# One int32 operation fewer in a reciprocal square root, and another choice of which score tiles VectorE exponentiates

## The chip, the cores and the metric

The kernel runs on one core of one Trainium2 chip. The time is that of the device, in microseconds, from the first to the last instruction and a little around it; lower is better. The engines that matter here are TensorE (PE in the profile; its weight loads are listed apart as PEld), ScalarE (ACT), VectorE (DVE), and SyncE (SP), whose queue issues the transfers.

## The reference

One block of a transformer on 2048 rows of 640 values in bfloat16: a layer norm, attention with 32 heads of 20 values each, a second layer norm, and a gated feed-forward layer of width 1728, each with its residual.

```python
def _layernorm(x, axis=-1, eps=1e-5):
    m = jnp.mean(x, axis=axis, keepdims=True)
    v = jnp.var(x, axis=axis, keepdims=True)
    return (x - m) / jnp.sqrt(v + eps)
...
        scores = jnp.einsum("bhqd,bhkd->bhqk", q, k) * (Dh ** -0.5)
        p = _softmax(scores, axis=-1)
        o = jnp.einsum("bhqk,bhkd->bhqd", p, v)
...
        h = _gelu(g) * u
        return jnp.einsum("bsf,fd->bsd", h, w_down)

    x = A_x
    h = x + _A_ref(_layernorm(x, axis=-1), A_wqkv, A_wo)
    h2 = h + _B_ref(_layernorm(h, axis=-1), B_w_gate, B_w_up, B_w_down)
```

The costly part is the softmax: 32 heads of 2048 x 2048 scores, each of which has to be exponentiated once. As tiles of 128 keys x 512 score columns that is 2048 tiles.

## The kernel before

**Chunks and slots.** The query rows are cut into seven chunks of 512, 512, 256, 256, 256, 128 and 128 rows (`CHUNKS`). The heads form eight groups of four. Attention is worked off in 32 slots of 64 score tiles each: a slot of chunk 0 or 1 is one group of heads, a slot of a 256-row chunk two groups, a slot of a 128-row chunk four. So slots 0 to 7 belong to chunk 0, 8 to 15 to chunk 1, 16 to 19, 20 to 23 and 24 to 27 to chunks 2, 3 and 4, 28 and 29 to chunk 5, and 30 and 31 to chunk 6.

**Units.** Within a slot, PE writes the scores of two or three tiles into neighbouring PSUM banks (function `unit`), and one ACT instruction exponentiates them together, 1024 or 1536 columns wide, into `pts` or `pts2` in SBUF. That is a unit. Two sets of banks are used in turn. A slot marked `2` in the string `PATS` alternates units of three tiles (banks 0 to 2) with units of two (banks 3 and 4). A slot marked `3` has units of three tiles in both sets (banks 0 to 2 and 3 to 5), and so takes bank 5 as well. Bank 6 gathers the product of probabilities and values. What is left, banks 7 and 5, or 7 alone in a slot marked `3`, serves all background work.

**VectorE's tiles.** In some units of three the third tile is not given to ACT but to VectorE (function `d_exp`). How many there are in each slot stands in the string `DS`, one hexadecimal digit per slot; they are spread evenly over the slot's three-tile units, leaving out the first and the last two. VectorE multiplies and clamps the 512 score columns into int16, which is a first approximation of the exponential's bfloat16 bits, and corrects them in a chain of seven operations over two such tiles at a time (over one, where a slot's number is odd). The product with the values then takes them up eight units later at the earliest.

**Background work.** Under all this run the projections of queries, keys and values (`proj`, `proj_v`), and for each finished chunk the function `post`: output projection, residual, layer norm statistics, `ln_rsqrt`, normalisation, transposes, the gate, the gelu, the up product and the down product. PE fills remaining time with matmuls that compute nothing (`idle`, from `gk`). Chunk 5 leaves its gelu, up and down work until the last exponential is done (`GT`). Chunk 6 has all its work after that: the tail.

**What sets the order.** `Sched` plans everything ahead with estimated durations and priorities: scores and their exponentials first, products with the values second, epilogues third, background last. The result is one fixed list of instructions for each engine, so each engine works strictly in that order, and an instruction whose input is late holds up all behind it. Any change of a number in `PATS` or `DS` gives a new plan for the whole kernel.

**The reciprocal square root.** `ln_rsqrt` has two branches. With `need_nm` (the first layer norm and the tail chunk) ACT takes a square root and VectorE a reciprocal. Without it (the second layer norm of chunks 0 to 5) VectorE does it alone for a chunk's one, two or four tiles of 128 rows at once: add epsilon, shift the bits right by one, subtract from a magic number, and two Newton steps of three operations each. That is nine operations on 1 to 4 columns.

Lines: most instructions go through the helper `I` and have line 386; 660 is a matmul in one piece (`whole`) and 664 one in four column groups (`quarters`); 618 and 952 are transposes; 749 copies projected values; 1081 copies gates, 1100 is the up product's multiplication and 1117 the down product's residual.

Of the kernel before, what the change touches and what calls it, by code (L numbers as in the profile page):

```python
# [6 lines left out]
ALU = mybir.AluOpType  # L7
# [3 lines left out]
I32 = mybir.dt.int32  # L11
# [39 lines left out]
class Sched:  # L51
# [10 lines left out]
    def op(self, eng, fns, dur, prio, reads=(), writes=(), acq=(), rel=(), after=(), sem=None, lat=None, mode=None, mb=0.0, alt=None):  # L62
        if self.evp is not None and eng == "dve" and rel and prio >= P_EPI:
            prio = self.evp
        o = Op()
        o.i = len(self.ops)
        o.eng, o.dur, o.lat, o.sem = eng, dur, LAT[eng] if lat is None else lat, sem
        o.mode = mode
        o.mb = mb
        o.alt = alt  # L70
        o.tag = writes[0] if writes else None
        o.fns = fns if isinstance(fns, list) else [fns]
        o.prio = (prio, o.i)
        deps = set(after)
        for r in reads:
            if r in self.lw:
                deps.add(self.lw[r])
        for w in writes:
            if w in self.lw:
                deps.add(self.lw[w])  # L80
            deps.update(self.rd.get(w, ()))
        for r in reads:
            self.rd.setdefault(r, []).append(o.i)
        for w in writes:
            self.lw[w] = o.i
            self.rd[w] = []
        deps.discard(o.i)
        o.deps = deps
        o.acq = list(acq)
        o.rel = list(rel)  # L90
        o.succ = []
        o.ready = 0.0
        o.start = None
        o.group = None
        self.ops.append(o)
        return o.i
# [230 lines left out]
RSQRT_MAGIC = float(0x5F3759DF)  # L327
# [25 lines left out]
XLAG = 0.85  # L353
XLG0 = 0.5
HG = 1
GT = (5,)
XPL = 1
KPR = 3.0
# [6 lines left out]
def bass_sequential_preLN__mha_block__glu_gated_geglu__prompt_kernel(  # L365
# [12 lines left out]
    with ExitStack() as es:  # L378
        sc = Sched(nc)
        op = sc.op  # L380
# [4 lines left out]
        def I(method, *args, **kwargs):  # L385
            return lambda eng: getattr(eng, method)(*args, **kwargs)  # L386


        def c_mm(n, passes=1):
            return 0.003 + passes * n / 2400.0  # L390
# [92 lines left out]
        def bank(b, n=512):  # L483
            return PS[:, 512 * b.b:512 * b.b + n]
# [91 lines left out]
        def ln_rsqrt(t0, n, prio, need_nm=0):  # L576
            ts = range(t0, t0 + n)
            y, v = rs[:, t0:t0 + n], mv[:, t0:t0 + n, 1]
            a, b = nw[:, 0, 0:n], nw[:, 1, 0:n]
            vk, rk = [("mv", t) for t in ts], [("rs", t) for t in ts]  # L580
            d = lambda fn, r, w: op("dve", fn, 0.14, prio, reads=r, writes=w)
            if need_nm:

                op("act", I("activation", a, v, ACT.Sqrt, bias=epsc[:, 0:1]), 0.19, prio, mode="sqrt", reads=vk + ["eps"], writes=["nw0", "sd"])
                d(I("reciprocal", y, a), ["nw0"], rk)
                if need_nm == 1:
                    d(I("scalar_tensor_tensor", out=nm[:, t0:t0 + n], in0=y, scalar=-1.0, in1=mv[:, t0:t0 + n, 0],
                        op0=ALU.mult, op1=ALU.mult), rk + vk, [("nm", t) for t in ts])
                return
            d(I("tensor_scalar", a, v, LN_EPS, None, ALU.add), vk, ["nw0"])  # L590
            d(I("tensor_scalar", b.bitcast(I32), a.bitcast(I32), 1, None, ALU.logical_shift_right), ["nw0"], ["nw1"])
            d(I("tensor_scalar", y.bitcast(I32), b.bitcast(I32), -1.0, RSQRT_MAGIC, ALU.mult, ALU.add), ["nw1"], rk)
            for _ in range(2):
                d(I("tensor_tensor", b, y, y, ALU.mult), rk, ["nw1"])
                d(I("scalar_tensor_tensor", out=b, in0=b, scalar=-0.5, in1=a, op0=ALU.mult, op1=ALU.mult),
                  ["nw0", "nw1"], ["nw1"])
                d(I("scalar_tensor_tensor", out=y, in0=b, scalar=1.5, in1=y, op0=ALU.add, op1=ALU.mult),
                  ["nw1"] + rk, rk)

        def ln_apply(eng, src, dst, dkey, t, rkeys, prio):  # L600
# [32 lines left out]
        def sc_id():  # L633
            _id[0] += 1
            return _id[0]
# [4 lines left out]
        for t0 in range(0, NT, 4):  # L640
            sa = [t for t in range(t0, t0 + 4) if LNS[t] == "act"]
            for t in range(t0, t0 + 4):
                (ln_stats_act if t in sa else ln_stats)(x_sb[:, t, :], t, [xkey(t)], P_EPI)
            if sa:
                assert sa == list(range(sa[0], sa[-1] + 1))
                op("dve", I("tensor_scalar", mv[:, sa[0]:sa[-1] + 1, 1], mv[:, sa[0]:sa[-1] + 1, 1], 1.0 / D, None, ALU.mult), 0.14,
                   P_QK, reads=[("mv1", t) for t in sa], writes=[("mv", t) for t in sa])
            ln_rsqrt(t0, 4, P_QK, 1)
            for t in range(t0, t0 + 4):
                e_ops.append(ln_apply(LNE[t], x_sb[:, t, :], xn_p[:, t % 4, :], ("xnp", t % 4), t, [xkey(t)], P_QK))  # L650
                transposes(xn_p[:, t % 4, :], [("xnp", t % 4)], xnT[:, :, t * 128:(t + 1) * 128], ("xnT", t),
                           ALLB, P_EPI, LNV[t])
                e_ops.append(len(sc.ops) - 2)
# [5 lines left out]
        def whole(out, l, r, start, stop):  # L659
            return [lambda eng: eng.matmul(out()[0:l.shape[-1]], l, r, start=start, stop=stop, skip_group_check=True)]  # L660

        def quarters(out, l, r, start, stop):
            m = l.shape[-1]
            return [lambda eng, j=j: eng.matmul(out()[j:j + 32], l[:, j:j + 32], r, start=start, stop=stop,  # L664
                                                tile_position=(0, j), skip_group_check=True) for j in range(0, m, 32)]
# [97 lines left out]
            tiles += [(s_, g, kb, j) for g in gs for kb in range(NT // nk) for j in range(4)]  # L763
            slot_end.append(len(tiles))

        PATS = '22222222222322232222222332223322'
        DS = '06418768558877797888786986867867'
        PAT = [((0, 1, 2), (3, 4, 5)) if PATS[i] == '3' else ((0, 1, 2), (3, 4)) for i in range(len(slots))]
        units, ubank, upos = [], [], []
        i = 0  # L770
# [154 lines left out]
        for s_, (c, gs) in enumerate(slots):  # L925
            us = [u for u, tl in enumerate(units) if len(tl) == 3 and all(x[0] == s_ for x in tl)]
            n = int(DS[s_], 16)
            us = us[1:len(us) - DTAIL]
# [50 lines left out]
        def post(c, banks, tail):  # L979
            p = P_EPI if tail else P_BG - PRE * (c >= PREC)  # L980
            q0, nq = CHUNKS[c]
# [10 lines left out]
            for tt in range(nt):  # L992
# [10 lines left out]
                for hf in range(2):  # L1003
                    bk = Bank(*banks)
# [11 lines left out]
            if tail:  # L1016
                op("act", I("activation", nm[:, 0:1], off0[:], ACT.Gelu_apprx_tanh), 0.06, -1, mode="gelu", reads=["off0"],
                   writes=["pre"], after=(sc.lw["sd"],))
# [5 lines left out]
            p, pre = P_BG - TFIRST * tail, p  # L1024
# [11 lines left out]
            def mms(k, w, wkey, after, p=p):  # L1036
                bk, key = Bank(*banks), ("bk", sc_id())
                for fi in range(min(fn_, NF - k * fn_)):
                    f = k * fn_ + fi
                    mf = min(128, DFF - 128 * f)  # L1040
                    for a in range(NA):
                        st = fi == 0 and a == 0
                        op("pe", quarters(lambda fi=fi: bank(bk)[:, fi * nq:(fi + 1) * nq], w[:, a, f * 128:f * 128 + mf],
                                          hnT[:, a, hb * 128:hb * 128 + nq], a == 0, a == NA - 1),
                           c_mm(nq), p, mode="col", alt=whole(lambda fi=fi: bank(bk)[:, fi * nq:(fi + 1) * nq],
                                                              w[:, a, f * 128:f * 128 + mf], hnT[:, a, hb * 128:hb * 128 + nq],
                                                              a == 0, a == NA - 1), reads=hk + [wkey], writes=[key], acq=[bk] if st else [],
                           after=after if st else ())
                return bk, key

            def wid(k):
                return min(512, NF * nq - 512 * k)
# [16 lines left out]
            else:  # L1069

                cp, gl = [], []
                for k in range(nb):
# [3 lines left out]
                    w_ = wid(k)  # L1076
                    if k >= nb - HG and c not in GT:
                        hold.append((k, bg, kg, m, fv, fk, w_))
# [3 lines left out]
                                 reads=[kg], writes=fk, rel=[bg], after=first))  # L1082
# [39 lines left out]

            if c in GT:
                def later(ba):
                    banks[:] = ba
                    gate_after[:] = [last_exp[0]]
                    rest()
                    down(GDP)
# [8 lines left out]
        if XPL:  # L1137
            op("act", I("activation", nm[:, 0:1], off0[:], ACT.Exp, scale=0.0), 0.06, P_QK, mode="exp", reads=["off0", ("xnT", 15), ("xnT", 14)],
               writes=["xpl", ("nm", 0)])
# [20 lines left out]
        for s_, (c, gs) in enumerate(slots):  # L1160
            if c == 0:
                g = s_
# [70 lines left out]
```

## Time and profile before

| | before |
|---|---|
| median of 3 runs | 939.43 us (938.72 to 939.80) |
| profiled execution, its own time | 939.73 us |
| its span, first to last instruction | 937.9 us |
| PE busy | 877.7 us (94%) |
| ACT busy | 904.2 us (96%) |
| DVE busy | 794.5 us (85%) |
| granted TensorE clock | 1.000 |

The profile's page lists busy times, groups of instructions by line, and who waited for whom. Two things have to be kept apart when it is read. The duration of an ACT instruction is longer than the time by which it moves its successor, because successive instructions overlap; the chain of work that ended last, in order of time, shows the latter. And an engine that is idle only costs time where it is the one on which the others depend at that moment. The slots can be found in the trace from the ACT instructions of 1024 and 1536 columns, which come in the units' order: slot 0 begins at 32.9 us, slot 31 at 880.4 us, and the last exponential ends at 908.4 us.

### The profile page before, as it was taken

The page shows a single profiled execution, that of the slowest core. Times are in us where ns is not written, and L with a number is a line of the kernel's source. Part 1 is how long each engine was busy: PE and PEld are TensorE (multiplying, and loading weights), DVE is VectorE, ACT ScalarE, POOL GpSimd, SP SyncE. Part 2 cuts the span into 40 slices and gives each one's busy share as a digit, 9 for nine tenths or more (in the row PEclk, how much of TensorE's full clock was granted, in tenths as well). Part 3 has the DMA queues.
Part 4 walks back from the last instruction along what each step waited for, and adds up shares of the span by engine and source line. Part 5 has one row for each costly group of instructions (what it writes and reads, how often), then busy time and mean ns, then how long its engine had stood idle before and what let it go on. Part 6 is the DMA issues. An engine that isn't in the chain of part 4 may idle for free.

```text
span 937.9 us, 33402 instructions
## 1 busy us (share of the span) xinstructions
PE 877.7 (94%) x15201; PEld 386.6 (41%) x15203; DVE 794.5 (85%) x1749; ACT 904.2 (96%) x884; POOL 11.2 (1%) x45
## 2 busy tenths in 40 slices
PE   5999999999999989999999999999889999989998
PEld 3433332222233222323343333344445654556666
DVE  8659768999999999688999996988998787898673
ACT  7999999999999999999999999999999999999891
POOL 4000000000000000000000000000000000000000
PEclk9999999999999999999999999999999999999999
DMA  7010000000000160000100000011000010000000
GB/s 253 2 30 2 2 1 2 1 1 2 1 2 2 33 253 2 1 1 17 43 3 1 2 2 2 2 31 26 7 3 3 3 31 17 17 4 3 5 18 15
DMA packets 11820, 19.90 MB, mean 21 GB/s; under 512 B 608, under 2 KB 9760, under 8 KB 11680
## 3 DMA queue, kind: packets, MB, share of 16 engines
q1 hardware_dynamic: 11680, 17.78, 5.7%
q8 instruction: 119, 1.95, 0.9%
q14 instruction: 21, 0.17, 0.1%
HBM read 15.16 MB, written 2.62 MB: 19 GB/s over the span
## 4 chain that ended last, share of the span: by engine, by line
ACT 74%; PE 20%; DVE 4%; POOL 1%; issue 1%; POOLq 0%
ACT pts L386 44%; ACT rege L386 29%; PE ps L664 7%; PE ps L386 7%; PE ps L660 4%; DVE rege L386 2%; PE ps L618 1%; POOL regw L386 1%; DVE stats L386 0%; DVE qt_all L386 0%; PE ps L952 0%; DVE rege L1100 0%; DVE kt_all L694 0%; ACT L1087 0%; ACT rege L1087 0%
## 5 line engine op out<-in xcount | busy, mean ns | idle before, releaser
L386 ACT ACTIVATE pts<-ps 128x1024 bf16<-128x1024 f32 (+1 forms) x482 | 549.3, 1345 | 3.2 <-PE ps L386 3.0
L386 ACT ACTIVATE rege<-ps 128x1024 bf16<-128x1024 f32 (+1 forms) x312 | 363.6, 1328 | 1.4 <-PE ps L386 1.3
L386 PE MATMUL ps<-qt_all,kt_all 32*128 32x256 bf16 (+2 forms) x3584 | 311.2, 288 | 36.1 <-ACT pts L386 16.4
L386 PEld LDWEIGHTS ps<-qt_all,kt_all 32*128 32x128 bf16 x3584 | 96.5, 92 | 275.8 <-ACT pts L386 130.6
L664 PE MATMUL ps<-rege,regw 128*32 128x256 bf16 (+2 forms) x2970 | 158.7, 308 | 5.1 <-issue 2.3
L386 PE MATMUL ps<-pts,v_all 128*21 128x256 bf16 (+2 forms) x1956 | 157.7, 292 | 0.4 <-DVE osb L386 0.3
L386 PE MATMUL ps<-rege,v_all 128*21 128x256 bf16 (+2 forms) x1394 | 129.4, 294 | 0.0
L664 PE MATMUL ps<-regw 128*32 128x512 bf16 (+1 forms) x1656 | 120.5, 358 | 1.0 <-DVE v_all L749 0.5
L386 DVE TENSOR_TENSOR rege<-rege 128x1024 bf16<-128x1024 bf16 (+3 forms) x170 | 108.4, 641 | 1.0
L386 DVE TENSOR_SCALAR qt_all<-ps 128x512 int16<-128x512 f32 x110 | 75.3, 685 | 16.0 <-PE ps L386 15.5
L664 PEld LDWEIGHTS ps<-rege,regw 128*32 128x32 bf16 x2970 | 73.3, 96 | 37.6 <-issue 17.5
L386 DVE TENSOR_SCALAR rege<-rege 128x1024 bf16<-128x1024 int16 (+3 forms) x225 | 87.3, 398 | 1.3
L386 DVE TENSOR_TENSOR qt_all<-qt_all 128x1024 bf16<-128x1024 bf16 (+3 forms) x124 | 82.3, 664 | 1.2
L664 PE MATMUL ps<-regw,rege 128*32 128x320 bf16 x1484 | 79.3, 301 | 0.3 <-DVE rege L1100 0.3
L386 DVE TENSOR_SCALAR rege<-ps 128x512 int16<-128x512 f32 x103 | 70.5, 684 | 9.0 <-PE ps L386 8.5
L386 DVE TENSOR_SCALAR qt_all<-qt_all 128x1024 bf16<-128x1024 int16 (+3 forms) x182 | 73.3, 408 | 1.9
L386 PEld LDWEIGHTS ps<-pts,v_all 128*21 128x21 bf16 x1956 | 46.4, 90 | 60.6 <-issue 52.5
L386 PEld LDWEIGHTS ps<-rege,v_all 128*21 128x21 bf16 x1394 | 38.4, 90 | 42.1 <-issue 35.1
L386 PE MATMUL ps<-wo,gk 128*21 128x256 bf16 x296 | 52.6, 274 | 0.0
L664 PEld LDWEIGHTS ps<-regw 128*32 128x32 bf16 x1656 | 37.8, 95 | 34.8 <-issue 15.9
L1100 DVE TENSOR_TENSOR rege<-rege,ps 128x512 bf16<-128x512 bf16 (+2 forms) x53 | 35.8, 676 | 13.1 <-PE ps L664 12.8
L664 PEld LDWEIGHTS ps<-regw,rege 128*32 128x32 bf16 x1484 | 35.8, 95 | 22.2 <-issue 13.7
(109 smaller groups left out, 727.3 us busy)
## 6 DMA issues: line engine op xcount, KB each, us to landing
rege<-in_A_x_dram SPq DMA_DIRECT2D x11, 320.0 KB, 4.7
out_dram<-rege SPq DMA_DIRECT2D x16, 160.0 KB, 1.9
regw<-in_B_w_gate_dram SPq DMA_DIRECT2D x1, 2160.0 KB, 9.2
regw<-in_B_w_up_dram SPq DMA_DIRECT2D x1, 2160.0 KB, 14.1
regw<-in_B_w_down_dram SPq DMA_DIRECT2D x1, 2080.0 KB, 19.2
rege<-in_A_wqkv_dram SPq DMA_DIRECT2D x1, 1600.0 KB, 9.0
rege<-in_A_x_dram SPq DMA_DIRECT2D x2, 640.0 KB, 4.4
regw<-in_A_wqkv_dram SPq DMA_DIRECT2D x1, 800.0 KB, 8.0
```

The lines of the kernel that those rows point to most:

```text
L386: return lambda eng: getattr(eng, method)(*args, **kwargs)
L618: op("pe", lambda eng, a=a: eng.transpose(bank16(bk, D)[:, 128 * a:128 * a + 128], src[:, a * 128:(a + 1) * 128], ident[:]), 0.056, prio, ...
L660: return [lambda eng: eng.matmul(out()[0:l.shape[-1]], l, r, start=start, stop=stop, skip_group_check=True)]
L664: return [lambda eng, j=j: eng.matmul(out()[j:j + 32], l[:, j:j + 32], r, start=start, stop=stop, tile_position=(0, j), skip_group_check=T ...
L1100: hdone.append(op("dve", lambda eng, bu=bu, fv=fv, m=m, w_=w_: eng.tensor_tensor(fv, fv, bank(bu, w_)[0:m, :], ALU.mult), c_dve(w_), p, re ...
```

## The change

In `ln_rsqrt` the shift and the subtraction from the magic number become one operation: the bits, taken as a number, times -0.5 plus the magic number. This branch has eight operations instead of nine.

`PATS` marks slots 12 and 22 with `3` that were `2`, and slot 29 with `2` that was `3`: seven slots of three-tile units instead of six. `DS` changes in ten slots: 1 (6 to 3), 2 (4 to 5), 10 (8 to 9), 13 (7 to 8), 15 (9 to 8), 20 (7 to 8), 22 (6 to 7), 24 (8 to 7), 27 (6 to 8) and 31 (7 to 8). In all VectorE takes 216 tiles instead of 213.

Three options are added and stay off: `LNG` (parts of the square root on GpSimd) with its `LNGT`, and `FW` (chunk 5's gates in one piece). With both at 0 the instructions they guard are those of before.

```diff
+LNG = 0
+LNGT = 0.2
+FW = 0
...
             d(I("tensor_scalar", a, v, LN_EPS, None, ALU.add), vk, ["nw0"])
-            d(I("tensor_scalar", b.bitcast(I32), a.bitcast(I32), 1, None, ALU.logical_shift_right), ["nw0"], ["nw1"])
-            d(I("tensor_scalar", y.bitcast(I32), b.bitcast(I32), -1.0, RSQRT_MAGIC, ALU.mult, ALU.add), ["nw1"], rk)
+            d(I("tensor_scalar", y.bitcast(I32), a.bitcast(I32), -0.5, RSQRT_MAGIC, ALU.mult, ALU.add), ["nw0"], rk)
+            if LNG:
+                g = lambda fn, r, w: op("pool", fn, LNGT, prio, reads=r, writes=w)
+            else:
+                g = d
             for _ in range(2):
-                d(I("tensor_tensor", b, y, y, ALU.mult), rk, ["nw1"])
-                d(I("scalar_tensor_tensor", out=b, in0=b, scalar=-0.5, in1=a, op0=ALU.mult, op1=ALU.mult),
+                g(I("tensor_tensor", b, y, y, ALU.mult), rk, ["nw1"])
...
+                g(I("scalar_tensor_tensor", out=b, in0=b, scalar=-0.5, in1=a, op0=ALU.mult, op1=ALU.mult),
                   ["nw0", "nw1"], ["nw1"])
-                d(I("scalar_tensor_tensor", out=y, in0=b, scalar=1.5, in1=y, op0=ALU.add, op1=ALU.mult),
+                g(I("scalar_tensor_tensor", out=y, in0=b, scalar=1.5, in1=y, op0=ALU.add, op1=ALU.mult),
                   ["nw1"] + rk, rk)
...
-        PATS = '22222222222322232222222332223322'
-        DS = '06418768558877797888786986867867'
+        PATS = '22222222222332232222223332223222'
+        DS = '03518768559878787888887976887868'
...
-                        op("pe", quarters(lambda fi=fi: bank(bk)[:, fi * nq:(fi + 1) * nq], w[:, a, f * 128:f * 128 + mf],
+                        wh = FW and c in GT
+                        op("pe", (whole if wh else quarters)(lambda fi=fi: bank(bk)[:, fi * nq:(fi + 1) * nq], w[:, a, f * 128:f * 128 + mf],
                                           hnT[:, a, hb * 128:hb * 128 + nq], a == 0, a == NA - 1),
-                           c_mm(nq), p, mode="col", alt=whole(lambda fi=fi: bank(bk)[:, fi * nq:(fi + 1) * nq],
+                           c_mm(nq), p, mode="full" if wh else "col", alt=None if wh else whole(lambda fi=fi: bank(bk)[:, fi * nq:(fi + 1) * nq],
```

More of the change, by code (lines that the diff above doesn't have):

```diff
@@ L590, in ln_rsqrt @@
             d(I("tensor_scalar", a, v, LN_EPS, None, ALU.add), vk, ["nw0"])
-            d(I("tensor_scalar", b.bitcast(I32), a.bitcast(I32), 1, None, ALU.logical_shift_right), ["nw0"], ["nw1"])
-            d(I("tensor_scalar", y.bitcast(I32), b.bitcast(I32), -1.0, RSQRT_MAGIC, ALU.mult, ALU.add), ["nw1"], rk)
-            for _ in range(2):
-                d(I("tensor_tensor", b, y, y, ALU.mult), rk, ["nw1"])
-                d(I("scalar_tensor_tensor", out=b, in0=b, scalar=-0.5, in1=a, op0=ALU.mult, op1=ALU.mult),
+            d(I("tensor_scalar", y.bitcast(I32), a.bitcast(I32), -0.5, RSQRT_MAGIC, ALU.mult, ALU.add), ["nw0"], rk)
[3 more added lines that the diff above has]
+                g = d
+            for _ in range(2):
+                g(I("tensor_tensor", b, y, y, ALU.mult), rk, ["nw1"])
+                if LNG:
+                    g(I("tensor_tensor", b, b, a, ALU.mult), ["nw0", "nw1"], ["nw1"])
+                    g(I("tensor_scalar", b, b, -0.5, 1.5, ALU.mult, ALU.add), ["nw1"], ["nw1"])
+                    g(I("tensor_tensor", y, y, b, ALU.mult), ["nw1"] + rk, rk)
+                    continue
+                g(I("scalar_tensor_tensor", out=b, in0=b, scalar=-0.5, in1=a, op0=ALU.mult, op1=ALU.mult),
                   ["nw0", "nw1"], ["nw1"])
-                d(I("scalar_tensor_tensor", out=y, in0=b, scalar=1.5, in1=y, op0=ALU.add, op1=ALU.mult),
+                g(I("scalar_tensor_tensor", out=y, in0=b, scalar=1.5, in1=y, op0=ALU.add, op1=ALU.mult),
                   ["nw1"] + rk, rk)
```

## The prediction

> **What bounds the kernel now.** I read the first part of the page, then who waited for whom on ACT between the first and last exponentials, then the chain of work in order of time, and last the busy times slot by slot.
>
> ```profile
> span 937.9 us, 33402 instructions
> PE 877.7 (94%) x15201; PEld 386.6 (41%) x15203; DVE 794.5 (85%) x1749; ACT 904.2 (96%) x884; POOL 11.2 (1%) x45
> ```
>
> ACT is the busiest engine. From 36.5 to 892 us its only waits for another engine are these (total us, times, longest):
>
> ```profile
> ACT pts L386 <- PE ps L386: 3.0, 3, 1.6
> ACT rege L386 <- PE ps L386: 1.3, 1, 1.3
> ```
>
> 4.3 us of 855: ACT sets the pace, and the attention phase ends when ACT has done its share of the 2048 score tiles. What a tile costs there is read from the chain (start, us, what), not from durations, because successive ACT instructions overlap:
>
> ```profile
> 98.55 2.75 ACT rege L386 x3
> 101.30 4.09 ACT pts L386 x4
> ...
> 114.01 3.60 ACT pts L386 x3
> ```
>
> Slot 2 begins at 89.8 and here has three 1024-column instructions in a row: 2.75 / 3 = 0.917 us each. The 4.09 holds three of these and one of 1536 columns: 4.09 - 2.75 = 1.34 us. Check: the 3.60 is one 1024 and two 1536, 0.917 + 2.68 = 3.60. The difference, 0.42 us, is one tile of 512; what remains of an instruction without its tiles is 0.917 - 0.84 = 0.07 us.
>
> The counts and durations by shape (us busy, mean ns):
>
> ```profile
> L386 ACT ACTIVATE pts<-ps 128x1024 bf16<-128x1024 f32 x322 | 347.3, 1202 | 1.6 <-PE ps L386 1.6
> L386 ACT ACTIVATE pts<-ps 128x1536 bf16<-128x1536 f32 x160 | 257.3, 1634 | 1.5 <-PE ps L386 1.4
> L386 ACT ACTIVATE rege<-ps 128x1024 bf16<-128x1024 f32 x225 | 245.4, 1208 | 1.4 <-PE ps L386 1.3
> L386 ACT ACTIVATE rege<-ps 128x1536 bf16<-128x1536 f32 x87 | 141.3, 1636 | 0.0
> ```
>
> 322 + 225 = 547 units of two tiles and 160 + 87 = 247 of three: 1094 + 741 = 1835 tiles, and 2048 - 1835 = 213 are VectorE's, the sum of the digits of `DS`.
>
> **Fewer tiles and instructions on ACT.** The new digits sum to 216, so ACT has 1832 tiles. The number of units follows from walking through the 64 tiles of each slot with the new pattern: a slot marked `2` takes 25.6 units, one marked `3` takes 21.3, and with seven marked `3` instead of six the walk gives 790 instead of 794. With n units of three, 3n + 2(790 - n) = 1832 gives n = 252, so 538 of two. ACT's change is 5 x 1.34 - 9 x 0.917 = 6.70 - 8.25 = -1.55 us. By the mean durations it would be 5 x 1.635 - 9 x 1.204 = -2.66; that counts overlap twice, so it is the far end of this term, and the near end is three tiles without any instruction saved, 3 x 0.42 = -1.26. I take -1.55, the chain's value.
>
> **Work put on VectorE.** A tile costs one operation on PSUM and its share of the chain of four `tensor_scalar` and three `tensor_tensor`:
>
> ```profile
> L386 DVE TENSOR_TENSOR rege<-rege 128x1024 bf16<-128x1024 bf16 x112 | 76.4, 684 | 0.8
> L386 DVE TENSOR_SCALAR qt_all<-ps 128x512 int16<-128x512 f32 x110 | 75.3, 685 | 16.0 <-PE ps L386 15.5
> ...
> L386 DVE TENSOR_SCALAR rege<-rege 128x1024 bf16<-128x1024 int16 x112 | 46.8, 419 | 1.0
> ```
>
> A chain over two tiles is 4 x 0.419 + 3 x 0.684 = 3.73 us. A further tile in a slot costs 0.69 us and, if it opens another pair, up to 3.73. Over the kernel there are 14 odd slots instead of 13 and 101 full pairs instead of 100, so VectorE gets 3 x 0.69 + 3.73 + at most 3.73, some 9.5 us. None of it is on the path while VectorE is in time. Whether it is, the busy times of the slots show (us of the slot, then PE, PEld, DVE and ACT busy with counts):
>
> ```profile
> 61.90:89.80 27.90, 25.93 (x372) 9.00 (x371) 24.57 (x54) 26.35 (x26) 0.00 (x0) 1.00 0.08 25
> 302.20:328.20 26.00, 24.57 (x256) 7.39 (x248) 25.29 (x52) 26.00 (x28) 0.00 (x0) 1.00 0.10 28
> 568.00:602.70 34.70, 32.73 (x542) 12.92 (x539) 26.75 (x53) 34.64 (x34) 0.00 (x0) 1.00 0.01 2
> 628.90:655.90 27.00, 26.54 (x541) 12.33 (x530) 22.38 (x57) 26.83 (x27) 0.00 (x0) 1.00 0.09 22
> 770.30:795.90 25.60, 25.22 (x564) 12.71 (x556) 19.36 (x37) 25.60 (x27) 0.00 (x0) 1.00 0.09 27
> 880.40:908.40 28.00, 25.66 (x857) 16.45 (x846) 21.71 (x46) 25.50 (x27) 0.00 (x0) 1.00 0.04 10
> ```
>
> These are slots 1, 10, 20, 22, 27 and 31. Where tiles are added VectorE is free for 7.9 us (slot 20), 4.6 (22), 6.2 (27, which gets two: 2 x 0.69 + 3.73 = 5.1) and 6.3 (31). Only slot 10 is full: 0.7 us free against 0.69 plus an added half chain. Its background copies wait into later slots, which I cost at nothing as long as scores don't need them.
>
> **The wait in slot 1.** The longest of ACT's waits stands at the end of slot 1:
>
> ```profile
> 89.83 2.37 ACT L386 ACTIVATE pts<-ps 128x1024 bf16<-128x1024 f32 x2 [1.58 <-PE ps L386]
> ```
>
> On PE and VectorE just before it:
>
> ```profile
> 88.94 0.40 PE L386 MATMUL ps<-rege,v_all 128*21 128x512 bf16 x4
> 89.15 0.32 PE L664 MATMUL ps<-regw 128*32 128x320 bf16 x4
> 89.40 0.40 PE L386 MATMUL ps<-qt_all,kt_all 32*128 32x512 bf16 x4
> ```
> ```profile
> 88.16 0.41 DVE L386 TENSOR_SCALAR rege<-rege 128x1024 int16<-128x1024 int16 x1
> ```
>
> The scores that ACT needs (89.40) stand in PE's list behind the slot's last products with values (88.94), and these need VectorE's chain, whose last operation ends at 88.57. VectorE was late because slot 1 had 24.57 us of work in 27.9. The change takes three of its six tiles, 3 x 0.69 + one pair and more, over 5.8 us. I take it that the chain is then done in time and the whole 1.58 us goes: -1.58. The bounds are 0 (the next late input is right behind it) and -1.58, since ACT had no work ready. What is late next there is PE itself, 25.93 us busy in 27.9; but slot 1 also has 1.3 us more of ACT's tiles, so PE gets that much longer.
>
> **The background's banks.** A slot marked `3` leaves the background one bank instead of two. What this costs PE can be read from the filler matmuls, busy time of those that read `gk` (first number after the slot's us; all fillers from slot 10 on):
>
> ```profile
> 352.90:379.40 26.50, 0.27 (x1) 0.09 (x1) 0.00 (x0) 1.00 0.00 1
> 491.40:517.30 25.90, 8.24 (x45) 3.44 (x45) 0.00 (x0) 1.00 0.01 2
> 628.90:655.90 27.00, 0.97 (x8) 0.61 (x9) 0.00 (x0) 1.00 0.09 22
> 795.90:822.30 26.40, 4.28 (x26) 2.01 (x26) 0.00 (x0) 1.00 0.06 16
> 822.30:847.20 24.90, 5.44 (x35) 2.73 (x34) 0.00 (x0) 1.00 0.02 4
> ```
>
> Slots 12 and 22, now `2`, have almost no filler; slots 28 and 29, now `3`, have 4.3 and 5.4 us. So turning a slot to `3` puts off some 4 us of PE's background work. Slot 12's is caught up in slot 17, where 8.24 us are filler. Slot 22's 3.3 to 4.5 us come back in slot 29, which turns to `2` and stops wasting 5.4. Net between -2 and +4 us of work left for the tail; I take 0, as the loss and the gain are of one size.
>
> **The square root.** One operation goes in each of six chunks:
>
> ```profile
> L386 DVE TENSOR_SCALAR nw<-nw 128x2 int32<-128x2 int32 x3 | 0.5, 163 | 0.0
> L386 DVE TENSOR_SCALAR nw<-nw 128x4 int32<-128x4 int32 x2 | 0.3, 160 | 0.0
> L386 DVE TENSOR_SCALAR nw<-nw 128x1 int32<-128x1 int32 x1 | 0.2, 154 | 0.0
> ```
>
> 6 x 0.16 = 1.0 us of VectorE in the background, hidden by ACT's exponentials; the tail's chunk takes the other branch. The merged operation is of the kind that stays, so it costs no more. I take 0 on the path, bounds 0 and -1.0. The options that stay off add nothing, and no transfer and no wait on SP or POOL moves.
>
> **PE's own stalls in the last slot.** ACT's other two long waits, in slot 31, follow gaps on PE in which it waited for no semaphore:
>
> ```profile
> 881.93 0.34 PE L664 MATMUL ps<-rege,regw 128*32 128x128 bf16 x9 [0.87 <-issue]
> ...
> 885.68 0.23 PE L664 MATMUL ps<-rege,regw 128*32 128x128 bf16 x1 [1.13 <-issue]
> ```
> ```profile
> 882.65 1.45 ACT L386 ACTIVATE pts<-ps 128x1536 bf16<-128x1536 f32 x1 [1.22 <-PE ps L386]
> ```
>
> The second costs ACT the 1.3 us of the waits above, so 2.5 together. They fall in a run of the shortest instructions, chunk 5's gates, 857 matmuls in slot 31 against 372 in slot 1, and that work stays there. I keep both: 0; bounds -2.5 and, if a third gap joins, +1.3.
> The Trainium skill (Runtime: NRT & Kernel Launch, section Instruction fetch mechanics) has PE's instructions fetched in blocks of 256 while the block before runs, and the crossing "mostly hidden". By that rule such gaps are no fixed price of short instructions, and the sum would be 2.5 us lower; the trace here leaves open which holds.
>
> **The sum.** 939.73 - 1.55 - 1.58 = 936.6 us, against the profiled execution, which lies 0.3 above the median of the runs; the runs spread by 1.1. I forecast 936.6.
>
> **The rivals.** (a) The wait in slot 1 stays or turns up at another slot's end, such as slot 10, where VectorE is full. For it: the pace is set by fixed lists, and one late input is enough. Against it: no other slot's end shows such a wait, slot 10's included. The time is 939.73 - 1.55 = 938.2. (b) The stalls of the last slot go with the new order as well: 936.6 - 2.5 = 934.1. For it: nothing but PE's own timing holds them there. Against it: the same short work falls in the same slots. (c) Slower: the bank taken in slots 12 and 22 leaves background for the tail, where it is in PE's way, since a part of the down products spills over already. From 908.4 us on PE runs
>
> ```profile
> L660 PE MATMUL ps<-regw,rege 128*128 128x320 bf16 x70 | 11.3, 300 | 0.5 <-DVE rege L1100 0.5
> ```
>
> 14 f-blocks by two halves are 28 for chunk 6 and 28 for chunk 5, so 14 of them, half a tile of rows and 2.3 us, are chunk 4's. If slot 22's 4 us come at the end in full, 936.6 + 4 = 940.6; if slot 12's 4 us come too, 944.6. It decides against the change once the spill passes 3.1 us, and can be measured as slower past 4.7 (936.6 + 4.7 = 941.3). Against it: slot 17's fillers and slot 29's second bank. That the change does not do what it says can't be: the counts follow from the strings.
>
> **How the numbers follow.** Chances: the forecast 0.45, (a) 0.24, (b) 0.17, (c) 0.14, with most of (c) past 941.3. About 0.2%, 1.9 us, can be told from no change: below 937.5 is faster, above 941.3 slower. Faster: the forecast and (b), 0.62, less a little for the forecast's own upper end: 0.60. Slower: 0.13. The same: 0.27. The range leaves out the far part of (c), 0.13, and a few in a hundred below: 933.4, which is every one of ACT's waits gone (939.73 - 1.55 - 4.3 = 933.9) and half of the square root's 1.0, up to 941.0.
>
> **What would show it.** Right: 538 ACT instructions of 1024 columns and 252 of 1536, 216 operations from PSUM to int16 on VectorE, no int32 shift; no ACT wait near 90 us; the last exponential some 3 us before 908.4 and a tail of 29.5 us as before. Wrong: ACT waits for scores at a slot's end elsewhere (a); PE's gaps gone or more (b); fewer fillers in slots 15 to 17, many more matmuls in the tail, which is longer by their time (c).

## The result, and the profile after

The changed kernel takes 937.39 us (median of 20 runs, 936.71 to 940.13) against 939.64 us for the kernel before, measured beside it. The ratio is 0.9979, with a 95% interval of 0.9973 to 0.9986: 2 us faster, a little more than can be told from no change. The forecast was 936.6. The profiled execution took 936.72 us, among the quickest of the 20, with a span of 934.9; so the profiles differ by 3.0 us and the medians by 2.25. One of the 20 runs of the kernel before took 3993.75 us, and one of 27 in a later round 1011.99; both are left out of the ratios.

The changed kernel's page, span and busy times, then ACT's waits between the first and the last exponential (total us, times, longest):

```profile
span 934.9 us, 33351 instructions
PE 876.2 (94%) x15171; PEld 385.8 (41%) x15173; DVE 798.1 (85%) x1760; ACT 902.4 (97%) x880; POOL 11.1 (1%) x45
```
```profile
ACT pts L389 <- PE ps L389: 1.3, 1, 1.3
ACT rege L389 <- PE ps L389: 0.9, 2, 0.5
```

ACT waited 4.3 us before and 2.2 now. Its exponentials by shape (the helper's line is now 389):

```profile
L389 ACT ACTIVATE pts<-ps 128x1024 bf16<-128x1024 f32 x331 | 358.2, 1220 | 1.4 <-PE ps L389 1.3
L389 ACT ACTIVATE pts<-ps 128x1536 bf16<-128x1536 f32 x154 | 250.6, 1661 | 0.1
L389 ACT ACTIVATE rege<-ps 128x1024 bf16<-128x1024 f32 x207 | 227.7, 1217 | 0.0
L389 ACT ACTIVATE rege<-ps 128x1536 bf16<-128x1536 f32 x98 | 159.2, 1666 | 0.9 <-PE ps L389 0.9
```

331 + 207 = 538 and 154 + 98 = 252, as worked out. The 1.58 us wait near 90 us is gone. What the scores behind it waited for, before (the weight load of these scores, then VectorE):

```profile
89.40 0.11 PEld L386 LDWEIGHTS ps<-qt_all,kt_all 32*128 32x128 bf16 x5 [0.34 <-DVE qt_all L733]
88.50 0.74 DVE L733 SCALAR_TENSOR_TENSOR qt_all<-ps,khalf,qt_all 128x512 bf16<-128x512 f32 x1
```

and after:

```profile
89.16 0.09 PEld L389 LDWEIGHTS ps<-qt_all,kt_all 32*128 32x128 bf16 x2 [0.27 <-DVE qt_all L744]
88.28 0.75 DVE L744 SCALAR_TENSOR_TENSOR qt_all<-ps,khalf,qt_all 128x512 bf16<-128x512 f32 x1 [0.36 <-PE ps L675]
```

They waited for the last operation on the next slot's queries (line 733, now 744), which stood in VectorE's list right behind the chain of its tiles. Slot 1 after (us of the slot, then PE, PEld, DVE, ACT busy):

```profile
61.90:89.60 27.70, 27.20 (x409) 9.75 (x401) 19.69 (x46) 27.57 (x27) 0.00 (x0) 1.00 0.07 25
```

VectorE has 19.69 us of work there instead of 24.57, and now waits 0.36 us for PE before that operation. So the queries are ready only 0.2 us sooner (89.03 instead of 89.24), and slot 2 begins at 89.6 instead of 89.8. The rest of the wait is filled, not saved in place: ACT has three tiles more to do in slot 1, 1.26 us, and fewer in other slots. The last exponential ends at 904.4 us instead of 908.4, 4.0 earlier; but the tail behind it takes 30.5 us instead of 29.5. In the chain of work in order of time (start, us, what), before:

```profile
909.49 1.06 PE ps L660 x7
910.54 0.45 PE ps L952 x4
```

and after:

```profile
905.68 1.67 PE ps L671 x10
907.36 0.44 PE ps L963 x4
```

The tail's first transposes (952, now 963) stand behind ten matmuls of chunk 4's down product instead of seven, and begin 2.96 us after the last exponential instead of 2.14. That is 0.8 of the 1.0 us.

### The profile page after: what moved, and what is told of

Its sections match the earlier page's. It is cut to its first block, busy times and chain, and to the rows that moved or that the text cites. A ratio compares the mean times of both kernels' runs of the same rounds, so it can differ in the third digit from the quotient of the medians.

```text
span 934.9 us, 33351 instructions
## 1 busy us (share of the span) xinstructions
PE 876.2 (94%) x15171; PEld 385.8 (41%) x15173; DVE 798.1 (85%) x1760; ACT 902.4 (97%) x880; POOL 11.1 (1%) x45
## 4 chain that ended last, share of the span: by engine, by line
ACT 83%; PE 12%; DVE 4%; POOL 1%; issue 1%; POOLq 0%
ACT pts L389 50%; ACT rege L389 32%; PE ps L671 4%; PE ps L675 4%; PE ps L389 3%; DVE rege L389 1%; DVE qt_all L389 1%; PE ps L629 1%; POOL regw L389 1%; DVE rege L1093 0%; DVE stats L389 0%; ACT L389 0%; ACT L1099 0%; PE ps L963 0%; ACT rege L1099 0%
## 5 line engine op out<-in xcount | busy, mean ns | idle before, releaser
L675 PE MATMUL ps<-rege,regw 128*32 128x256 bf16 (+2 forms) x2970 | 160.7, 308 | 3.4 <-DVE qt_all L744 0.8
L389 PE MATMUL ps<-rege,v_all 128*21 128x256 bf16 (+2 forms) x1396 | 127.5, 294 | 0.0
L389 DVE TENSOR_TENSOR rege<-rege 128x1024 bf16<-128x1024 bf16 (+2 forms) x172 | 111.7, 652 | 0.9
L389 DVE TENSOR_SCALAR qt_all<-qt_all 128x1024 int16<-128x1024 int16 (+3 forms) x187 | 74.0, 402 | 1.5
L675 PE MATMUL ps<-regw,rege 128*32 128x320 bf16 (+1 forms) x1452 | 71.9, 301 | 0.4 <-DVE rege L1129 0.3
L675 PEld LDWEIGHTS ps<-regw,rege 128*32 128x32 bf16 (+1 forms) x1452 | 35.0, 96 | 20.6 <-issue 9.9
```

## The experiments

What is compared throughout is the median and the ratio to the kernel before, measured on the same chip. Two numbers tell where time went: when the last exponential ends, and how many matmuls of 320 columns (down products) are left after it; 56 of them belong there, chunk 5's and 6's. Slot 0 begins between 32.5 and 33.7 us in these profiles, so a difference below 1 us in the fourth column says little by itself; and the intervals of the ratios are some 0.9 us to either side for most rows.

| kernel | us | ratio, interval | last exp. ends | 320-column matmuls after it |
|---|---|---|---|---|
| before | 939.6 | | 908.4 | 70 |
| changed | 937.4 | 0.9979 (0.9973 to 0.9986) | 904.4 | 78 |
| merged operation alone | 940.5 | 1.0010 (1.0001 to 1.0019) | 908.6 | 70 |
| new strings, old square root | 947.3 | 1.0083 (1.0069 to 1.0096) | 903.7 | 112 |
| merged, new PATS, old DS | 942.0 | 1.0026 (1.0016 to 1.0035) | 911.0 | 56 |
| merged, old PATS, new DS | 946.4 | 1.0073 (1.0061 to 1.0086) | 907.4 | 112 |
| changed, with six shifts more | 937.4 | 0.9983 (0.9974 to 0.9992) | - | - |
| changed, slot 29 as before | 938.5 | 0.9992 (0.9984 to 1.0001) | 905.8 | 94 |
| changed, slots 1 and 2 as before | 938.5 | 0.9984 (0.9975 to 0.9993) | 904.9 | 78 |
| changed, gates whole | 935.3 | 0.9956 (0.9943 to 0.9968) | 902.4 | 83 |
| before, gates whole | 937.1 | 0.9973 (0.9964 to 0.9983) | 906.2 | 73 |

**The merged operation alone.** The change's `ln_rsqrt` with the strings of before.

```diff
-        PATS = '22222222222332232222223332223222'
-        DS = '03518768559878787888887976887868'
+        PATS = '22222222222322232222222332223322'
+        DS = '06418768558877797888786986867867'
```

> The kernel before with the merged int32 operation alone; the strings PATS and DS as before. Chain theory (the step as predicted): VectorE has 1.0 us less work in the background under ACT, ACT has the same 794 instructions, the wait of 1.58 us near 88 us stays because chunk 0's square root comes only after slot 7. Ratio to before 0.9995 to 1.0005, within 0.5 us. Rival (the plan is what matters): six shorter operations give another plan from slot 8 on, and waits, PE gaps or the spill into the tail move by a microsecond or more: a ratio outside 0.999 to 1.001.

Measured: 940.5 us, ratio 1.0010 (1.0001 to 1.0019), on the edge between the theory's range and the rival's. One operation fewer did not make the kernel faster; by the medians it made it 0.9 us slower, barely clear of the noise. The new plan has two waits on ACT in slot 12 that the kernel before does not have:

```profile
357.52 1.02 ACT L389 ACTIVATE pts<-ps 128x1024 bf16<-128x1024 f32 x1 [0.34 <-PE ps L389]
359.35 1.02 ACT L389 ACTIVATE rege<-ps 128x1024 bf16<-128x1024 f32 x1 [0.80 <-PE ps L389]
```

**The strings alone.** The kernel before with the new PATS and DS.

```diff
-        PATS = '22222222222322232222222332223322'
-        DS = '06418768558877797888786986867867'
+        PATS = '22222222222332232222223332223222'
+        DS = '03518768559878787888887976887868'
```

> The kernel before with the new PATS and DS and the old nine-operation square root. Chain theory: the same 790 ACT instructions as in the changed kernel (538 and 252), slot 1's wait mostly gone, so all of the gain: ratio 0.9979 within 0.0007, last exponential ending 904 to 905.5 us. Rival (the strings were searched for the plan with the merged operation, and fit only that): the ratio lies nearer to 1, 0.999 or more, with waits in ACT after slot 8 that the changed kernel does not have.

Measured: 947.3 us, 7.7 us slower than before and nearly 10 slower than the changed kernel, from whose code it differs by one operation of 0.16 us in six chunks. The rival had the direction, but not the place: ACT's phase ends even earlier, at 903.7 us, and the loss stands in the tail (us busy, mean ns):

```profile
L660 PE MATMUL ps<-rege,regw 128*128 128x128 bf16 (+3 forms) x283 | 20.7, 229 | 0.0
L660 PE MATMUL ps<-regw,rege 128*128 128x320 bf16 x112 | 17.2, 300 | 0.0
```

Against 210 and 78 in the changed kernel: a good part of chunk 4's up product and all of its down product (56) are left over, and run on PE before and between chunk 6's own work. The background is late from chunk 1 on. That chunk's first normalisations in the changed kernel and in this one:

```profile
515.55 0.80 DVE L389 TENSOR_SCALAR xn_t<-rege,mv,rs 128x640 bf16<-128x640 bf16 x2
```
```profile
532.31 0.44 DVE L386 TENSOR_SCALAR xn_t<-rege,mv,rs 128x640 bf16<-128x640 bf16 x1
```

17 us late there, and not caught up: chunk 4's first normalisation comes at 849.1 us instead of 822.3.

**The operation's work, or the plan?** The changed kernel with the old pair of operations, the shift planned at no time, so that every engine's list stays and VectorE's has six shifts more.

```diff
-            d(I("tensor_scalar", y.bitcast(I32), a.bitcast(I32), -0.5, RSQRT_MAGIC, ALU.mult, ALU.add), ["nw0"], rk)
+            op("dve", I("tensor_scalar", b.bitcast(I32), a.bitcast(I32), 1, None, ALU.logical_shift_right), 0.0, prio, reads=["nw0"], writes=["nw1"], lat=-0.03); d(I("tensor_scalar", y.bitcast(I32), b.bitcast(I32), -1.0, RSQRT_MAGIC, ALU.mult, ALU.add), ["nw1"], rk)
```

> The changed kernel with the old pair of operations (shift, then -1.0 times and the magic number) put back, but the shift planned at a duration of zero, so that the lists of PE, ACT, POOL and SP stay as in the changed kernel and VectorE's list has six shifts more and is otherwise the same. Theory P (the plan decides, the operation itself is worth nothing): 937.4 us within 0.6, ratio 0.998, tail of 30 us. Theory W (the work decides: VectorE is so full that 1.0 us of it in the background costs many): near the 947 us of the kernel with the old square root and the new strings, at least 940.

Measured: 937.37 us against the changed kernel's 937.39. The traces show the same lists on PE (but for a few missing records), ACT and GpSimd, and on VectorE the same list with six shifts more. Theory P holds: the six operations cost nothing that can be measured (the interval is some 0.9 us to either side), and what the merged one does to the time it does through the plan. (The execution that was profiled took 940.15 us, far above this median; the last section shows what was different in it, and its two numbers are left out of the table.)

**One string at a time, both with the merged operation.** First the new PATS with the old DS, then the old PATS with the new DS.

```diff
-        DS = '03518768559878787888887976887868'
+        DS = '06418768558877797888786986867867'
```
```diff
-        PATS = '22222222222332232222223332223222'
+        PATS = '22222222222322232222222332223322'
```

> The merged operation and the new PATS with the old DS (213 tiles, one slot more with three-tile units). Chain arithmetic: three tiles more on ACT than in the changed kernel, +1.3 us, slot 1's wait back, +1.1: 939.8 us. If the plan decides: background that is early or late by more than that, 938 or less, or 941 or more, to be seen in the matmuls after the last exponential.

> The merged operation and the new DS with the old PATS (216 tiles, slots 12 and 22 of two- and three-tile units, slot 29 of three-tile units). Chain arithmetic: four ACT instructions more than in the changed kernel, +0.3 us: 937.7 us. If the plan decides: outside 936.7 to 938.7, to be seen in the matmuls after the last exponential.

Measured: 942.0 and 946.4 us. Both lie outside what the chain arithmetic gives, the second by nearly 9 us. With the new DS alone, chunk 4's whole down product is left over once more:

```profile
L671 PE MATMUL ps<-regw,rege 128*128 128x320 bf16 x112 | 17.5, 300 | 0.0
```

With the new PATS alone nothing is left over (56), and the loss lies in ACT's phase, where the waits grow instead of shrinking:

```profile
ACT pts L389 <- PE ps L389: 5.6, 8, 1.6
ACT rege L389 <- PE ps L389: 0.4, 1, 0.4
```

That is 1.7 us more than before, of a phase that ends 2.7 us later although its arithmetic is 0.3 us shorter (255 units of three, 535 of two: 8 x 1.34 - 12 x 0.917); 0.3 us of the remaining 1.3 is a later start of slot 0, and the rest is not explained.

**VectorE in slots 17 and 18.** The kernel with the strings alone (947.3 us), with 13 tiles instead of 16 in these two slots.

```diff
-        DS = '03518768559878787888887976887868'
+        DS = '03518768559878787678887976887868'
```

> The kernel with the old square root and the new strings (947.3 us), but slots 17 and 18 with 6 and 7 tiles on VectorE instead of 8 and 8. There VectorE was 98 and 95% busy and chunk 1's layer norm came 20 us later than in the changed kernel. Theory V (that stretch of full VectorE makes the background late, and it is carried to the end): ACT gets three tiles more, +1.3 us, chunk 1's normalisation comes at least 10 us earlier, and the tail of 42 us falls to 30 to 36: 938 to 943 us. Rival C (the order of the plan, not VectorE's load there): chunk 1 stays late or another chunk becomes late, tail still 38 us or more, 945 to 949.

Measured: 945.3 us, ratio 1.0068 (1.0054 to 1.0082). The time is in the rival's range, the tail of 36.0 us at the edge of theory V's. The 98 and 95% in the expectation are slots 17 and 18 of the changed kernel; in the one meant here VectorE was busy for

```profile
490.30:516.20 25.90, 24.07 (x438) 10.62 (x438) 23.09 (x50) 25.90 (x27) 0.00 (x0) 1.00 0.06 22
516.20:540.90 24.70, 22.05 (x316) 9.68 (x316) 24.24 (x64) 24.70 (x26) 0.00 (x0) 1.00 0.01 2
```

89 and 98%. Chunk 1's normalisation comes earlier, as theory V has it:

```profile
519.51 0.80 DVE L386 TENSOR_SCALAR xn_t<-rege,mv,rs 128x640 bf16<-128x640 bf16 x2
```

12.8 us earlier. Chunk 4's first normalisation comes at 826.4 us instead of 849.1, its up product is no longer left over (210 matmuls of 128 columns in the tail instead of 283), and the tail shrinks by 6.0 us. But 112 down matmuls are left over all the same, chunk 4's 56 among them, and ACT's phase ends 3.7 us later where its tiles explain 1.3. So three tiles fewer in these slots bring the background forward. That it was VectorE's load is not shown: the changed kernel's VectorE is busier in the two slots (25.32 + 23.39 us against 23.09 + 24.24), and its chunk 1 is on time. What holds back chunk 4's down product was not found.

**Slot 29's bank.** The changed kernel with slot 29 marked `3`, as it was.

```diff
-        PATS = '22222222222332232222223332223222'
+        PATS = '22222222222332232222223332223322'
```

> The changed kernel with slot 29 marked 3 again (eight slots of three-tile units). Bank theory (as predicted): the background has one bank there, PE's fillers in slot 29 rise from 16 to some 60 rows, chunk 4's down products spill into the tail by 4 us more, ACT has 4 instructions less (-0.2 us): 3 to 5 us slower than the changed kernel, 940 to 942, with over 20 matmuls of 320 columns more after the last exponential. Rival: chunk 4 is limited by something else than banks (its own chain, VectorE), and the time stays within 1 us of 937.4.

Measured: 938.5 us, ratio 0.9992 (0.9984 to 1.0001): 1.1 us slower than the changed kernel, between the two. Filler in slot 29, and down products after the last exponential:

```profile
818.90:844.90 26.00, 4.03 (x23) 1.72 (x23) 0.00 (x0) 1.00 0.06 16
```
```profile
L671 PE MATMUL ps<-regw,rege 128*128 128x320 bf16 x94 | 15.0, 300 | 0.0
```

The changed kernel has 1.7 us of filler there and 78 such matmuls. The bank theory is right in kind: 2.3 us more of PE is idled away and 16 matmuls more (15.0 against 12.6 us) are left over. The bank is worth about half of the 4 us expected. The loss of 1.1 us is smaller still, and the two intervals (0.9984 to 1.0001, and 0.9973 to 0.9986) overlap a little. In the profiles the tail takes 32.3 us instead of 30.5, and ACT waits 1.1 us more, all of it at PE's gaps near the end, which the last section shows.

**Slots 1 and 2, both ways.** The changed kernel with the old digits there, and the kernel before with the new ones.

```diff
-        DS = '03518768559878787888887976887868'
+        DS = '06418768559878787888887976887868'
```
```diff
-        DS = '06418768558877797888786986867867'
+        DS = '03518768558877797888786986867867'
```

> The changed kernel, but slots 1 and 2 with 6 and 4 tiles on VectorE again (218 tiles in all). Chain theory: ACT has two tiles less than the changed kernel, -0.85 us, and the wait at the end of slot 1 comes back, +1.0 to +1.6 us: 0.2 to 0.8 us slower than the changed kernel, ratio to before 0.998 to 0.999, an ACT wait over 1.2 us near 88 us. Rival (the wait in slot 1 is not VectorE's load but where the plan happens to put the products): no wait over 0.7 us there, and the kernel is about 0.85 us faster than the changed one, ratio 0.997.

> The kernel before with 3 and 5 tiles on VectorE in slots 1 and 2 alone (211 tiles). Chain theory: ACT gets two tiles more, +0.85 us, and the wait of 1.58 us falls to 0.5 or less, -1.1 to -1.6 us: ratio 0.9990 to 0.9998. Rival (the wait only moves to another place, or was no cost): the kernel is 0.8 us slower than before, ratio 1.0009.

Measured: 938.5 and 940.7 us. In the first, the wait is back, to the hundredth:

```profile
89.43 2.36 ACT L389 ACTIVATE pts<-ps 128x1024 bf16<-128x1024 f32 x2 [1.58 <-PE ps L389]
```

It is the only wait that ACT has up to 460 us, and the kernel is 1.1 us slower than the changed one, a little over the 0.2 to 0.8 expected; the intervals of the two ratios overlap, so the size is not certain. In the second, the wait near 90 us is gone, and a new one stands in slot 15, where nothing was edited:

```profile
443.15 2.37 ACT L386 ACTIVATE pts<-ps 128x1536 bf16<-128x1536 f32 x2 [1.62 <-PE ps L386]
```

Ratio 1.0011 (1.0002 to 1.0020): the rival's number, by another place. So the six tiles on VectorE in slot 1 cause that wait: in all 13 profiles it stands (1.58 or 1.59 us) in the five with the digits 6 and 4 in slots 1 and 2, and in none of the eight with 3 and 5. And a wait that is removed can come up elsewhere.

**PE's gaps in the last slot.** The changed kernel with its option `FW` on, and the kernel before with the same edit: chunk 5's gates as 70 whole matmuls instead of 280 in column groups. Each matmul has its own weight load, so PE has 420 instructions less, not only the 210 matmuls that the expectation names.

```diff
-FW = 0
+FW = 1
```

> The changed kernel with FW at 1: chunk 5's gates as 70 matmuls in one piece instead of 280 in column groups, so PE has 210 instructions less in the last two slots. Theory I (PE's gaps in the last slot come with the rate of its instructions): the gaps of about 1 us on PE between 875 and 890 us go, and ACT's 1.3 us with them: 936 us or less, ratio 0.9965 or less. Rival (the gaps have another cause, or the switch between whole and grouped matmuls costs as much): an ACT wait over 1 us stays in the last slot and the time is within 1 us of 937.4 or above.

> The kernel before with chunk 5's gates as 70 matmuls in one piece instead of 280 in column groups, and nothing else. In the profiles the gaps on PE in the last slot stand exactly 256 instructions apart. Theory I (PE runs out of fetched instructions where it does over 256 of them in 3.75 us): both gaps and ACT's waits of 1.22 and 1.27 us go, 936.5 to 937.5 us, ratio 0.997 to 0.998, and the runs lie closer together. Rival (the gain of the changed kernel with whole gates came from its new plan): gaps or other waits stay, 938.5 us or more.

Measured: 935.3 us (935.15 to 935.39, five runs) and 937.1 us (936.71 to 937.71). Theory I holds twice: neither profile has a gap on PE without a releaser ("issue") between 870 and 892 us. All of ACT's waits in the exponential phase with the gates whole, in the changed kernel and in the one before:

```profile
ACT rege L389 <- PE ps L389: 0.4, 1, 0.4
```
```profile
ACT pts L386 <- PE ps L386: 1.8, 2, 1.6
```

The 1.6 of the second is slot 1's, the 0.4 of the first stands at 765 us, at the end of slot 26; the two of 1.22 and 1.27 us are gone. PE's matmuls and weight loads (counts in the third and fourth column) in the same 15 us from 875 on, changed kernel and gates whole:

```profile
875.00:890.00 15.00, 13.23 (x528) 9.43 (x516) 9.39 (x19) 13.28 (x14) 0.00 (x0) 1.00 0.02 5
```
```profile
875.00:890.00 15.00, 14.73 (x409) 10.27 (x407) 11.21 (x23) 15.00 (x16) 0.00 (x0) 1.00 0.02 4
```

This edit to the kernel before gains as much as the whole change does, and on top of the change it is the fastest kernel of the study, 0.44% under before. The spread of its runs falls from 3.4 us (20 runs) to 0.2 (five).

## Why the prediction was right, and where it was not

- **ACT's tiles and instructions (-1.55): right.** 538 and 252 as worked out, and the chain's prices, not the durations: those even rose, from 1634 to 1661 ns for 1536 columns, while the phase became shorter.
- **The wait in slot 1 (-1.58): right in size and in the tiles that cause it, wrong in how it goes.** Taking the tiles away removes it and putting them back restores 1.58 us. But the scores waited for the next slot's queries (line 733), not for the chain and its products with values, and these come only 0.2 us sooner. The wait goes because ACT has 1.26 us more to do until then; the gain is that those tiles are missing from slots where ACT never waited.
- **Waits elsewhere (not in the sum): +0.27.** A new wait of 0.44 us stands at 765 us, at the end of slot 26, and one of 0.17 at 630 us is gone.
- **VectorE's added work (0): right.** Its busy time rose by 3.6 us (794.5 to 798.1), less than the 9.5 - 1.0 worked out; the scores of the one new wait were held by ACT, not by VectorE.
- **The square root (0): right only with the lists held fixed.** Six shifts more in the same lists cost nothing (937.37). But the step was priced as an instruction and is a change of plan. On the old strings it costs 0.9 us; on the new ones its absence costs 10.
- **PE's gaps (0): they stay, a little shorter.** 2.49 us of ACT's waits in slot 31 before, 1.25 + 0.47 = 1.72 after, so -0.77.
- **The background's banks (0, bounds -2 to +4): the mis-sized term.** What is left for the tail came out at +1.0 us, 78 down matmuls instead of 70; that is what the profile's gain of 3.0 lacks to the 4.0 by which the last exponential moved. The price of a bank, some 4 us of filler a slot, was too high. After the change the fillers in slots 12, 22 and 29 are

```profile
351.80:378.40 26.60, 2.20 (x14) 1.14 (x14) 0.00 (x0) 1.00 0.01 2
626.90:652.00 25.10, 2.15 (x12) 0.95 (x12) 0.00 (x0) 1.00 0.08 22
818.60:844.50 25.90, 1.70 (x8) 0.59 (x8) 0.00 (x0) 1.00 0.10 29
```

So the two slots that lost a bank have 1.9 and 1.2 us more, and slot 29, which got one back, 3.7 less. By these three slots alone less would be left over, not more; that the order of the new plan makes up the rest is argued, not tried by itself. With the strings alone the tail is 12.5 us longer, 42.0 us (945.7 - 903.7), with the same banks as in the changed kernel.

In all, -1.55 - 1.58 + 0.27 - 0.77 + 1.0 is -2.6, of -3.0 in the profiles; the other 0.4 is in a start 0.1 us earlier and in delays that these views don't show. The median lies 0.7 above the profiled execution, which is one of the quickest. That the terms put at nothing nearly cancel is luck: none of them was worked out from the new plan, and in neighbouring plans they come to several us.

Of the rivals, (c) named what decides the slowest runs, background left over for the tail, and gave it 0.14. The forecast came true for this combination of operation and strings, but it added up terms that do not add: merged operation +0.9, strings +7.7, both -2.2. Of the five combinations measured (operation, strings, operation with either string, all), only the full one is faster than before. What the prediction left without a price is that every edit gives a new plan; and with PE at 94%, ACT at 96 and VectorE at 85% a plan's lateness can be carried to the end, as with the strings alone.

## What to carry to other kernels

Where lists are planned ahead and all engines are nearly full, price an edit as the plan it produces, not as the instructions it adds or removes; to tell the two apart, put the instructions back at a planned duration of zero, so that only the work changes. Read the backlog, what of the background is left when the bounding engine has finished, next to the bounding engine's own time: with the strings alone ACT finished 4.7 us sooner and the tail took 12.5 us longer. And before tuning the order further, look for stalls that no semaphore explains; here an option that the changed code leaves off was worth as much as the whole change.

## What the hardware showed that was not expected

**PE stops 256 instructions apart.** The gaps on PE near the end, in the kernel with slot 29 as before:

```profile
873.79 1.01 PE L675 MATMUL ps<-rege,regw 128*32 128x128 bf16 x40 [0.43 <-issue]
877.54 0.57 PE L675 MATMUL ps<-rege,regw 128*32 128x128 bf16 x28 [0.85 <-issue]
881.55 0.35 PE L675 MATMUL ps<-rege,regw 128*32 128x128 bf16 x12 [1.40 <-issue]
```

and what PE does between the last two, with its counts:

```profile
877.54:881.55 4.01, 2.62 (x128) 2.02 (x128) 1.89 (x3) 2.37 (x3) 0.00 (x0) 1.00 0.02 4
```

128 matmuls and 128 weight loads, 256 instructions. In the other profiles that have several such gaps in the last slots they are 253 to 257 recorded instructions apart, or twice that. PE has 30404 of them in the kernel before, and the profile's page counts the packets that bring them:

```profile
q8 instruction: 119, 1.95, 0.9%
```

30404 / 256 = 118.8, and in all 13 profiles the packets are the recorded instructions by 256, rounded up (117 to 120). So a packet brings 256 instructions. Neighbouring gaps end 3.5 to 4.0 us apart, however little PE has to do in between (2.6 us here). The packets' times fit a wait for the next block: in the kernel before, PE goes on at 881.93 and at 885.68 us, and between the two a packet begins at 883.10, 1.17 us after the first, and has landed at 884.40, 1.28 us before the second. Short matmuls in column groups, each with its own weight load, reach this rate; 420 instructions fewer ended the gaps. The Trainium skill (Runtime: NRT & Kernel Launch, section Instruction fetch mechanics) has blocks of 256 instructions, the next fetched while the current one runs, and calls the crossing "mostly hidden". The trace agrees with the size. With the gates whole the crossings are hidden here; at the rate of the grouped gates they are not, and a gap takes 0.3 to 1.4 us.

**The clock fell in some executions.** In the 940.15 us execution with the six shifts (same PE list as the changed kernel), the granted clock, the third number from the right:

```profile
880.00:885.00 5.00, 3.87 (x172) 3.05 (x168) 1.94 (x4) 3.65 (x4) 0.00 (x0) 1.00 0.03 7
885.00:890.00 5.00, 5.00 (x124) 3.32 (x116) 4.03 (x9) 3.74 (x4) 0.00 (x0) 0.53 0.02 5
890.00:895.00 5.00, 4.87 (x119) 2.80 (x118) 3.50 (x9) 4.33 (x5) 0.00 (x0) 0.79 0.01 3
```

After gaps on PE of 0.53, 0.64 and 1.13 us it falls to 0.53 for a while, and the execution is 3.5 us longer than the quickest of that kernel. Of the 31 executions of this PE list three had a mean clock of 0.996, at 940.1 to 940.8 us; the changed kernel with whole gates took no more than 935.39 in five. That the gaps cause the drop is not shown: the changed kernel's profiled execution has the same gaps of 0.64 and 1.13 us, the one with slot 29 as before even one of 1.40, and their clock stayed at 1.00.
